# Attention and SwiGLU in one kernel: the first block takes its last pair late, and requests go ahead of staging copies

## The chip, the cores and the metric

The kernel runs on one core of a Trainium2 chip. The metric is device time in microseconds of the whole kernel. TensorE (PE) multiplies, VectorE (DVE) and ScalarE (ACT) work elementwise, GpSimd (POOL) copies within on-chip memory and asks for transfers, SyncE (SP) asks for other transfers, among them transposing ones. [...]

## The reference

Attention over 8 batches of 12 heads, 448 positions, 64 numbers per head; its output, heads side by side (3,584 rows of 768), goes through a gated feed-forward layer.

```python
scores = scale * np.matmul(q, k.transpose(0, 1, 3, 2))      # 8 x 12 x 448 x 448
attn = softmax(scores)
x = np.matmul(attn, v) -> (3584, 768)
g = x @ w_gate                                              # 768 x 1536
silu = g * (1.0 / (1.0 + np.exp(-g)))
out = (silu * (x @ w_val)) @ w_out                          # 1536 x 768
```

All inputs and the output are 32-bit floats; the kernel loads them as 16-bit floats (the conversion is done by the transfer).

## The kernel before

Heads are worked on in 48 pairs, six to a batch. A pair goes through these stages:

- **Loads.** `load_qk16` asks GpSimd's queue for queries and keys (L139), `load_v` for values (L156), `load_w` for parts of the three weights (L171). From pair 12 (`QUAD`) on, keys and values come in two requests each (`load_keys`, L127). The requests of one pair are called q14, k14, v12 and so on below; V3 stands for `load_v(9, 3)`, the values of pairs 9 to 11 in one request, and g, v, o are quarters of the gate and value weights and halves of the output weights.
- **Turning queries and keys.** Up to pair 10, TensorE transposes them (`turn`, L243). From pair 11 on, `prep` and `prep_quad` (L184, L199) let GpSimd copy keys and queries into a staging tile `qk16` (three buffers) and then ask SyncE's queue for transposing transfers into `qkT` (five buffers).
- **Scores.** `qk(pr, c)` multiplies (L293; L262 and L275 from pair 12 on) and ScalarE takes the exponential. Each pair has four chunks; from pair 12 on, two pairs have seven, the fourth (`RU`) holding the rest of both.
- **Values.** `copy_v` (L167) copies values on VectorE into a tile with a column of ones; `pv` multiplies (L319, L327; L356 from pair 12 on), and VectorE divides by the sum (L338, L340; L397, L398) into `xt`.
- **X.** `turn_x` transposes `xt` into the feed-forward input `X`: up to pair 11 on TensorE with a VectorE copy (L427, L434), later by a transposing transfer (L436).
- **Feed-forward.** Eight blocks of 384 or 512 rows. `ffn1_steps` (L460) has 12 steps, each with a gate group `gp` of 6 matmuls, a tanh on ScalarE (L480), a value group `vp` of 6 matmuls and two VectorE operations (L484, L487). `ffn2_steps` (L492) multiplies by the output weights in groups of 12 matmuls (L510).

PSUM holds three wide tiles (`ps_s`, two banks each) for scores and most gate groups, and two narrow ones (`ps_f`, one bank each) for everything else.

The order is written by hand. A first loop runs the 24 score chunks of pairs 0 to 5. The main loop then goes through `plan`, whose steps x hold two or three chunks and the pairs whose values are due. In the steps that matter here, the chunks are: x = 0 pair 6 (two chunks), x = 4 pair 8, x = 5 the last of pair 8 and two of pair 9, x = 6 pair 9 and the first of pair 10, x = 8 three of pair 11, x = 9 the last of pair 11 and two of pair 12, x = 10 two of pair 12 (one is the rest of 12 and 13) and one of pair 13, x = 11 two of pair 13 and one of pair 14.

When a step enters a pair `pr`, it prepares a later pair and asks for others: at pair 8 `prep(11)` and q14, k14; at pair 9 `prep(12)`, `prep(13)`, then q15, k15 and v12; at pair 10 `prep(14)`, then q16, k16 and v13; and so on. Other requests come from a table by pair, `wq` (L568). At x = 0 the last pieces of pairs up to 5 are finished (`piece`), `turn_x(5)` follows, and `add_block(0, end)` opens the first block, of 384 rows, all from batch 0. A gate group takes a narrow tile instead of a wide one when `gate_small` is set, which a step without values due (`bare`) does.

Of the kernel before, what the change touches and what calls it, by code (L numbers as in the profile page):

```python
# [10 lines left out]
FP32 = mybir.dt.float32  # L11
# [9 lines left out]
LA = 6  # L21
RB = 5
FIRST = 6
# [14 lines left out]
def kernel(  # L38
# [11 lines left out]
    B, H, S, D = q.shape  # L50
# [4 lines left out]
    NCB = DM // 128  # L55
    NFB = DF // 128
    NHP = H // 2
    NPAIR = B * NHP
# [29 lines left out]
    ps_f = ctx.enter_context(tc.tile_pool(name="ps_f", bufs=2, space=PSUM))  # L88
# [67 lines left out]
    def load_v(pr, n=1):  # L156
        b, h = divmod(2 * pr, H)
        if pr >= QUAD:
            vd = vraw[:, ds(pr % VS, n)].rearrange("p r h c d -> p (r h) (c d)")
            load_keys(nc.gpsimd, vd, v, 2 * pr, 2 * n)  # L160
            return
        nc.gpsimd.dma_start(
            vraw[0:P, ds(pr % VS, n)].rearrange("p r h c d -> p (r h) (c d)"),
            v[b, h : h + 2 * n].rearrange("h (p c) d -> p h (c d)", c=NC),
        )
# [291 lines left out]

    gate_small = [False]

    def ffn1_steps(kk, c0, n, hts):  # L460
        for fb in range(NFB):

            def group(kind, dst):
                for cb in range(NCB):
                    nc.tensor.matmul(  # L465
                        dst[:, 0:n],
                        lhsT=wslice(kind, fb, cb),
                        rhs=X[kk][:, cb, ds(c0, n)],
                        start=(cb == 0),
                        stop=(cb == NCB - 1),  # L470
                    )

            if gate_small[0]:
                gate_small[0] = False
                gp = ps_f.tile([128, 512], FP32, tag="f", name="gp")
            else:
                gp = ps_s.tile([128, 2, 512], FP32, tag="s", name="gp")[:, 0]
            group("g", gp)
            sg = fp.tile([128, 512], FP32, tag="sg")
            nc.scalar.activation(sg[:, 0:n], gp[:, 0:n], AF.Tanh, scale=0.5)  # L480
            vp = ps_f.tile([128, 512], FP32, tag="f", name="vp")
            group("v", vp)
            t1 = fp.tile([128, 512], FP32, tag="t1")
            nc.vector.scalar_tensor_tensor(  # L484
                t1[:, 0:n], sg[:, 0:n], 1.0, gp[:, 0:n], ALU.add, ALU.mult
            )
            nc.vector.scalar_tensor_tensor(  # L487
                hts[:, fb, 0:n], t1[:, 0:n], 0.5 * HS, vp[:, 0:n], ALU.mult, ALU.mult
            )
            yield  # L490

    def ffn2_steps(kk, c0, n, hts, first, last_block):  # L492
        chunks = range(n // 128)
        if first:
            steps = [(ch, oh) for oh in range(2) for ch in chunks]
        else:
            steps = [(ch, oh) for ch in chunks for oh in range(2)]
        osbs = {}
        for ch, oh in steps:
            last = last_block and ch == n // 128 - 1  # L500
            if last or oh == 0:
                osbs[ch] = fp.tile([128, DM], FP32, tag="osb", bufs=3, name="osb")
            osb = osbs[ch]
            parts = [(oh * OH, OH)]
            if last and oh:
                parts = [(OH, OH // 2), (OH + OH // 2, OH // 2)]
            for m0, w in parts:
                op = ps_f.tile([128, 512], FP32, tag="f")
                for fb in range(NFB):
                    nc.tensor.matmul(  # L510
                        op[:, 0:w],
                        lhsT=hts[:, fb, ts(ch, 128)],
                        rhs=wo[oh][:, fb, ds(m0 - oh * OH, w)],
                        start=(fb == 0),
                        stop=(fb == NFB - 1),
                    )
                nc.scalar.activation(osb[:, ds(m0, w)], op[:, 0:w], AF.Copy, scale=1.0 / HS)  # L517
                if not last:
                    m0, w = 0, DM
                    if oh == 0:  # L520
                        continue
                l0 = c0 + ch * 128
                l = l0
                while l < l0 + 128:
                    b, j = divmod(l, S)
                    turned = D if b + NB * kk < QUAD // NHP else 0
                    c, p0 = divmod((j + turned) % S, P)
                    m = min(P - p0, l0 + 128 - l, (MQ if turned and j < MQ else S) - j)
                    eng = nc.scalar if last and m < 64 else nc.sync
                    eng.dma_start(  # L530
                        out[ts(NB * kk + b, S), :].rearrange("(p c) m -> c p m", c=NC)[
                            c, p0 : p0 + m, ds(m0, w)
                        ],
                        osb[l - l0 : l - l0 + m, ds(m0, w)],
                    )
                    l += m
            yield NFB * OH / 2400.0

    def block(i):
        kk, odd = divmod(i, 2)  # L540
        c0, n = (384, 512) if odd else (0, 384)
        hts = hp_.tile([128, NFB, 512], FP16, tag="h")
        return ffn1_steps(kk, c0, n, hts), ffn2_steps(kk, c0, n, hts, i == 0, i == B - 1), n

    with tc.manual_schedule():
        load_qk32(0)
# [4 lines left out]
        for vo in Vts:  # L551
# [17 lines left out]
            0: [("qk", 6), ("g", 0), ("v", 0)],  # L569
            1: [("V", 2), ("qk", 8, 1), ("g", 1), ("v", 1)],  # L570
            3: [("qk", 9, 1), ("qk", 10), ("g", 2), ("v", 2)],
            4: [("g", 3), ("v", 3), ("qk", 12)],
            6: [("V", 3), ("o", 0)],
            7: [("o", 1)],
        }

# [75 lines left out]
        def piece():  # L652
            pv_chunk(*pieces.pop(0))

        for u in range(FIRST * NC):
            pr, c = divmod(u, NC)
# [33 lines left out]
        g = FIRST * NC  # L690
        last = len(units)
        while g < last or queue:
            n = 2 if g < WIDE * NC else 3
            todo = []
# [16 lines left out]
        for x, (chunks, todo) in enumerate(plan):  # L711
            quads = [u for u in chunks if u[0] >= QUAD and u[1] == RU]
            for pr, c in quads + [u for u in chunks if u not in quads]:
                qk(pr, c)
            for _, p0 in todo:
                if p0 >= QUAD:
                    pv_piece(p0, RU)
            end = min([y for y in adds if y > x] + [len(plan) + 1])
            if x == 0:
                turn_x(4)  # L720
                while pieces:
                    piece()
                turn_x(5)
                add_block(0, end)
            for p0 in vcopies.get(x, []):
                copy_v(p0)
            entered = [pr for pr, c in chunks if c == 0]
            for pr in entered:
                lead = [pr + 3] if pr + 3 < QUAD else [pr + 3, pr + 4] if pr + 3 == QUAD else [pr + 4]
                for p in lead:  # L730
                    if NPE <= p < NPAIR:
                        prep(p)
                if 14 <= pr + LA < NPAIR:
                    load_qk16(pr + LA, 1)
                if 12 <= pr + 3 < NPAIR:
                    load_v(pr + 3)
            for pr, c in chunks:
                if c == 2 and pr < NPE - 2:
                    prep(pr + 2)()
            if x in adds and x > 0:  # L740
                add_block(adds[x], end - x, x)
            for _, p0 in todo:
                pv(p0)
                if p0 < XPE:
                    turns.append(p0)
                else:
                    turn_x(p0)
            for pr in entered:
                for w in wq.pop(pr, []):
                    emit(w)  # L750
            bare = not todo and bool(chunks)
            if adds[max(y for y in adds if y <= x)] < 2:
                if bare and oq and not fvq:
                    carry -= run_o()
                elif bare:
                    gate_small[0] = True
                carry = run_budget(left() / (end - x) + carry)
            else:
                nf, no = steps.pop(0) if steps else (0, 0)
                if bare and no:  # L760
                    run_o()
                    no -= 1
                elif bare:
                    gate_small[0] = True
                for y in range(nf):
                    if fvq:
                        run_fv()
                for _ in range(no):
                    run_o()
            if x == 1:  # L770
                turn_rests(0)
            while turns:
                turn_x(turns.pop(0))
            if XPE - 1 in [p0 for _, p0 in todo]:
                turn_rests(1)
# [39 lines left out]
```

The softmax here doesn't subtract the row's maximum and nothing guards it: scores larger than these inputs give would overflow.

## Time and profile before

| | |
|---|---|
| time, median of 3 (lowest to highest) | 452.88 us (452.05 to 453.5) |
| span of the profiled run | 450.3 us, mean TensorE clock 0.999 |
| packets over the DMA queues | 108,494, 49.90 MB |
| GpSimd's queue (software) | 46,832 packets, 24.56 MB |
| SyncE's queue (hardware) | 61,520 packets, 24.66 MB |
| longest wait of GpSimd in sum | 96.5 us in 20 waits, staging copies at L188, for transposes into qkT |

The page of the profile gives the busy time of each engine as a share of the span, and a picture of 40 equal slices of about 11.3 us, one digit for each in tenths. The answers on waits name an instruction group, what released it, the total in us, the number of waits and the longest. In a timeline each line has a start and a length in us; in brackets stands the idle time of the engine before it and what seems to have ended it. For a wait on several semaphores the last one to come is named, which is not always the one that was missing.

### The profile page before, as it was taken

What the parts mean: (1) busy time and instruction counts of PE and PEld (TensorE: products, weight loads), DVE (VectorE), ACT (ScalarE), POOL (GpSimd) and SP (SyncE); (2) the same over time, 40 slices, a digit from 0 to 9 for tenths busy, and PEclk for the clock granted to TensorE, in tenths of its full rate; (3) what the DMA queues carried; (4) which work ended last, traced back from release to release, by engine and by line L of the source; (5) the groups of instructions that cost most, each with busy time, mean ns of one, the idle gap of its engine ahead of it and who ended that gap; (6) DMA issues with size and microseconds to landing.
All of it is one profiled execution on the core that took longest, in us unless ns stands there. A gap on an engine that the chain in (4) does not pass through costs nothing.

```text
span 450.3 us, 9959 instructions
## 1 busy us (share of the span) xinstructions
PE 438.5 (97%) x4024; PEld 247.0 (55%) x4024; DVE 199.9 (44%) x447; ACT 224.8 (50%) x332; POOL 180.4 (40%) x299
## 2 busy tenths in 40 slices
PE   8999999799999999999999999999999999999996
PEld 3655565444456566554556556554455656644464
DVE  4666562455564354344444434344544434045400
ACT  6965667545663654455536365454454651222222
POOL 8755715997786464336453366423000000000000
PEclk9999999999999999999999999999999999999999
DMA  9999999999998699975985797955141211200033
GB/s 137 182 199 201 199 177 144 138 160 217 135 148 104 110 144 124 125 115 69 120 109 105 111 140 96 151 84 94 32 79 47 52 41 22 80 27 1 0 107 105
DMA packets 108494, 49.90 MB, mean 111 GB/s; under 512 B 60832, under 2 KB 104992, under 8 KB 108448
## 3 DMA queue, kind: packets, MB, share of 16 engines
q0 software_dynamic: 46832, 24.56, 47.7%
q1 hardware_dynamic: 61520, 24.66, 29.0%
q8 instruction: 31, 0.51, 0.5%
q14 instruction: 15, 0.12, 0.1%
q10 hardware_dynamic: 96, 0.05, 0.0%
HBM read 49.55 MB, written 11.01 MB: 134 GB/s over the span
## 4 chain that ended last, share of the span: by engine, by line
PE 82%; DMA 9%; DVE 4%; ACT 2%; issue 1%; POOL 1%; SPq 0%; DVEq 0%; POOLq 0%
PE op L510 23%; PE gp L465 23%; PE vp L465 19%; PE acc L356 8%; DMA k<-in_k_dram 5%; PE s L262 4%; DMA q<-in_q_dram 2%; DVE t L484 2%; DVE hts L487 2%; PE s L293 1%; ACT sg L480 1%; PE acc L319 1%; DMA vraw<-in_v_dram 1%; PE s L275 1%; PE tp L252 1%
## 5 line engine op out<-in xcount | busy, mean ns | idle before, releaser
L465 PE MATMUL gp<-X,wg 128*128 128x384 f16 (+1 forms) x576 | 124.7, 353 | 0.0
L465 PE MATMUL vp<-X,wv 128*128 128x384 f16 (+1 forms) x576 | 124.6, 352 | 0.0
L510 PE MATMUL op<-wo,hts 128*128 128x384 f16 (+1 forms) x684 | 115.5, 323 | 1.4 <-DVE xt L398 1.4
L283 ACT ACTIVATE E<-s 128x896 f16<-128x896 f32 x126 | 106.5, 922 | 14.4 <-PE s L262 9.2
L484 DVE SCALAR_TENSOR_TENSOR t<-sg,gp 128x384 f32<-128x384 f32 (+1 forms) x96 | 59.6, 621 | 119.4 <-ACT sg L480 119.4
L480 ACT ACTIVATE sg<-gp 128x384 f32<-128x384 f32 (+1 forms) x96 | 52.6, 548 | 92.9 <-PE gp L465 91.4
L510 PEld LDWEIGHTS <-hts 128*128 128x128 f16 x684 | 65.9, 98 | 46.6 <-issue 2.2
L465 PEld LDWEIGHTS <-wv 128*128 128x128 f16 x576 | 56.3, 98 | 52.6
L517 ACT ACTIVATE osb<-op 128x384 f32<-128x384 f32 (+1 forms) x57 | 27.6, 484 | 103.5 <-PE op L510 99.7
L465 PEld LDWEIGHTS <-wg 128*128 128x128 f16 x576 | 53.4, 98 | 45.5 <-issue 0.7
L487 DVE SCALAR_TENSOR_TENSOR hts<-t,vp 128x384 f16<-128x384 f32 (+1 forms) x96 | 59.6, 621 | 10.8 <-PE rtp L449 0.5
L188 POOL COPY qk<-k 128x512 f16<-128x512 f16 x36 | 22.9, 637 | 98.6 <-DMA qkT<-qk 96.5
L132 POOL DMA_DIRECT2D vraw<-in_v_dram x72 | 44.1, 637 | 14.9 <-DMA k<-in_k_dram 6.9
L356 PE MATMUL acc<-vo,E 128*128 128x65 f16 (+1 forms) x1152 | 43.0, 193 | 1.7 <-DVE hts L487 1.4
L301 ACT ACTIVATE E<-s 112x896 f16<-112x896 f32 x48 | 40.7, 917 | 7.8 <-PE s L293 7.5
L356 PEld LDWEIGHTS <-E 128*128 128x128 f16 (+1 forms) x1152 | 37.2, 96 | 12.8 <-issue 7.1
L132 POOL DMA_DIRECT2D k<-in_k_dram x70 | 42.5, 623 | 2.1 <-DMA wv<-in_moe_w_val_dram 0.7
L397 DVE RECIPROCAL R<-acc 128x4 f32<-128x4 f32 x68 | 12.1, 177 | 61.3 <-PE acc L356 61.2
L151 POOL DMA_DIRECT2D q<-in_q_dram x44 | 29.9, 678 | 5.0 <-PE s L293 1.6
L398 DVE TENSOR_TENSOR xt<-acc,R 128x256 f16<-128x256 f32 x68 | 28.9, 425 | 2.3
L262 PE MATMUL s<-qkT 64*128 64x448 f16 x216 | 28.1, 353 | 0.5 <-DMA qkT<-qk 0.5
L188 POOL COPY qk<-q 112x512 f16<-112x512 f16 x36 | 23.4, 651 | 0.0
(56 smaller groups left out, 185.4 us busy)
## 6 DMA issues: line engine op xcount, KB each, us to landing
vraw<-in_v_dram POOLq DMA_DIRECT2D x72, 64.0 KB, 4.8
q<-in_q_dram POOLq DMA_DIRECT2D x41, 112.0 KB, 3.7
k<-in_k_dram POOLq DMA_DIRECT2D x68, 64.0 KB, 4.5
wg<-in_moe_w_gate_dram POOLq DMA_DIRECT2D x8, 288.0 KB, 10.0
wv<-in_moe_w_val_dram POOLq DMA_DIRECT2D x8, 288.0 KB, 10.1
wo<-in_moe_w_out_dram POOLq DMA_DIRECT2D x2, 1152.0 KB, 20.1
out_dram<-osb SPq DMA_DIRECT2D x8, 288.0 KB, 3.7
out_dram<-osb SPq DMA_DIRECT2D x6, 336.0 KB, 2.9
```

Source lines behind the costliest of these rows:

```text
L132: eng.dma_start(dst[ts(s, 64)], rows)
L151: nc.gpsimd.dma_start(dst[0:P, ds(h0, 2 * n)], flat.rearrange("h (p c) d -> p h (c d)", c=NC))
L188: nc.gpsimd.tensor_copy(dst.rearrange("p c h d -> p h c d"), src)
L262: nc.tensor.matmul(s[:, hx, 0:S], lhsT=t[ts(hx, 64), ts(c + low(pr, hx), 128)], rhs=t[ts(hx, 64), ds(NC * 128, S)], start=True, stop=True,)
L283: nc.scalar.activation(e[:, 0 : 2 * S].rearrange("p (h q) -> p h q", h=2), s[:, :, 0:S], AF.Exp, scale=sm_scale)
L301: nc.scalar.activation(e[:, :, 0:S], s[0:P, :, 0:S], AF.Exp, scale=sm_scale)
L356: nc.tensor.matmul(accs[pr][0][hx][:, ts(j, D + 1)], lhsT=e[rows, ds(hx * S + j * 128, 128)], rhs=Vts[pr % NV][rows, hx, col, 0 : D + 1], ...
L465: nc.tensor.matmul(dst[:, 0:n], lhsT=wslice(kind, fb, cb), rhs=X[kk][:, cb, ds(c0, n)], start=(cb == 0), stop=(cb == NCB - 1),)
L480: nc.scalar.activation(sg[:, 0:n], gp[:, 0:n], AF.Tanh, scale=0.5)
L484: nc.vector.scalar_tensor_tensor(t1[:, 0:n], sg[:, 0:n], 1.0, gp[:, 0:n], ALU.add, ALU.mult)
L487: nc.vector.scalar_tensor_tensor(hts[:, fb, 0:n], t1[:, 0:n], 0.5 * HS, vp[:, 0:n], ALU.mult, ALU.mult)
L510: nc.tensor.matmul(op[:, 0:w], lhsT=hts[:, fb, ts(ch, 128)], rhs=wo[oh][:, fb, ds(m0 - oh * OH, w)], start=(fb == 0), stop=(fb == NFB - 1),)
```

## The change

It has three parts.

1. At x = 0, `turn_x(5)` is no longer ahead of the first block. The first step of `ffn1_steps` takes it in between: five of six gate matmuls (those that need pairs 0 to 4), `turn_x(5)`, five of six value matmuls, then the sixth of each. The first gate group takes a wide tile, since x = 0 no longer counts as bare. It is for the wait of TensorE for pair 5's division.
2. V3 is asked for at pair 4, ahead of q12 and k12, instead of at pair 6.
3. When a pair is entered, the requests for later queries, keys and values are written ahead of the staging copies of `prep`, so that the requests go out earlier.

```diff
-    def ffn1_steps(kk, c0, n, hts):
+    def ffn1_steps(kk, c0, n, hts, late=None):
...
-            def group(kind, dst):
-                for cb in range(NCB):
+            def group(kind, dst, cbs=range(NCB)):
+                for cb in cbs:
...
-            group("g", gp)
+            split = late and fb == 0
+            if split:
+                vp = ps_f.tile([128, 512], FP32, tag="f", name="vp")
+                group("g", gp, range(NCB - 1))
+                late()
+                group("v", vp, range(NCB - 1))
+                group("g", gp, [NCB - 1])
+            else:
+                group("g", gp)
             sg = fp.tile([128, 512], FP32, tag="sg")
             nc.scalar.activation(sg[:, 0:n], gp[:, 0:n], AF.Tanh, scale=0.5)
-            vp = ps_f.tile([128, 512], FP32, tag="f", name="vp")
-            group("v", vp)
+            if split:
+                group("v", vp, [NCB - 1])
+            else:
+                vp = ps_f.tile([128, 512], FP32, tag="f", name="vp")
+                group("v", vp)
...
+        late = (lambda: turn_x(FIRST - 1)) if i == 0 else None
...
-            4: [("g", 3), ("v", 3), ("qk", 12)],
-            6: [("V", 3), ("o", 0)],
+            4: [("g", 3), ("v", 3), ("V", 3), ("qk", 12)],
+            6: [("o", 0)],
...
-                turn_x(5)
                 add_block(0, end)
...
             for pr in entered:
+                if 14 <= pr + LA < NPAIR:
+                    load_qk16(pr + LA, 1)
+                if 12 <= pr + 3 < NPAIR:
+                    load_v(pr + 3)
                 lead = [pr + 3] if pr + 3 < QUAD else [pr + 3, pr + 4] if pr + 3 == QUAD else [pr + 4]
                 for p in lead:
                     if NPE <= p < NPAIR:
                         prep(p)
-                if 14 <= pr + LA < NPAIR:
-                    load_qk16(pr + LA, 1)
-                if 12 <= pr + 3 < NPAIR:
-                    load_v(pr + 3)
...
-            bare = not todo and bool(chunks)
+            bare = not todo and bool(chunks) and x > 0
```

More of the change, by code (lines that the diff above doesn't have):

```diff
@@ L542, in block @@
         hts = hp_.tile([128, NFB, 512], FP16, tag="h")
-        return ffn1_steps(kk, c0, n, hts), ffn2_steps(kk, c0, n, hts, i == 0, i == B - 1), n
+        late = (lambda: turn_x(FIRST - 1)) if i == 0 else None
+        return ffn1_steps(kk, c0, n, hts, late), ffn2_steps(kk, c0, n, hts, i == 0, i == B - 1), n
     with tc.manual_schedule():
```

## The prediction

> **What bounds the kernel now.** I read the shares of busy time first, then the slices, then TensorE's waits, and last the timelines of GpSimd and TensorE around the few places where TensorE stands still.
>
> ```profile
> PE 438.5 (97%) x4024; PEld 247.0 (55%) x4024; DVE 199.9 (44%) x447; ACT 224.8 (50%) x332; POOL 180.4 (40%) x299
> ...
> DMA  9999999999998699975985797955141211200033
> ```
>
> TensorE is busy for 97% of the 450.3 us span, so the whole idle time that a change can win is 11.8 us. The DMA row says where trouble can come from: the 16 DMA engines are full in the first 13 slices (up to about 70 us) and not after slice 21. The table by stretch confirms it: from 84 to 450 us TensorE is idle for 4.9 us in 366, from 72 to 84 us for 2.3 us in 12.
>
> ```profile
> PE op L510 <- DVE xt L398: 1.4, 1, 1.4
> PE acc L356 <- DVE hts L487: 1.4, 7, 0.2
> PE wp L116 <- DVE warm L547: 1.2, 1, 1.2
> PE acc L427 <- DVE xt L340: 1.0, 1, 1.0
> ...
> PE s L262 <- DMA qkT<-qk: 0.5, 1, 0.5
> ```
>
> Three of these waits matter here. The 1.0 us at L427 is `turn_x(5)` of step x = 0 waiting for the division of pair 5 (TensorE idle 28.7 to 29.66). The 0.5 us at L262 is the first score chunk of pair 14, waiting for a transpose at 80.58. The 1.4 us at L510 ends at 83.33: the output group needs the accumulator of pair 12, whose division sits on VectorE behind `copy_v(13)`, which waited for values until 81.81.
>
> GpSimd's timeline shows why those values are late (columns: start, length, engine, line, operation, idle before it and what ended it):
>
> ```profile
> 47.14 2.04 POOL L182 DMA_DIRECT2D wo<-in_moe_w_out_dram x2 [1.33 <-issue]
> 49.17 0.63 POOL L211 COPY qk<-q 112x512 f16<-112x512 f16 x1
> ...
> 53.41 0.61 POOL L188 COPY qk<-k 128x512 f16<-128x512 f16 x1 [0.77 <-DMA k<-in_k_dram]
> ...
> 56.36 1.20 POOL L132 DMA_DIRECT2D k<-in_k_dram x2
> 64.39 0.59 POOL L132 DMA_DIRECT2D vraw<-in_v_dram x1 [6.84 <-DVE R L338]
> 71.93 0.59 POOL L132 DMA_DIRECT2D vraw<-in_v_dram x1 [6.94 <-DMA k<-in_k_dram]
> 73.14 0.61 POOL L188 COPY qk<-k 128x512 f16<-128x512 f16 x1 [0.62 <-DMA k<-in_k_dram]
> ```
>
> The requests at 64.39 and 71.93 are the two halves of `load_v(12)`. The releasers named are not the cause. The two `wo` requests landed as follows (asked for at 47.14 and 48.17):
>
> ```profile
> wo<-in_moe_w_out_dram POOLq DMA_DIRECT2D x1, 1152.0 KB, 16.7
> wo<-in_moe_w_out_dram POOLq DMA_DIRECT2D x1, 1152.0 KB, 23.5
> ```
>
> That is 63.84 and 71.67: each half of v12 went out 0.3 to 0.5 us after one of them. Counting GpSimd's requests in order, `wo` 0 and 1 are numbers 44 and 45, v12's halves 52 and 53; the records name eight completion semaphores in turn, and earlier pairs fit (request 24 at 20.47 follows the landing of 16 at 20.2; 39 at 38.81 that of 31 at 38.5). So a request waits until the one eight before it has landed, and GpSimd, being in order, holds everything behind it. In the kernel before, only the copies of pair 14 were behind v12.
>
> [...] while transposes ran (54 to 62 us) the software queue moved about 0.145 MB/us, without them 0.197. [...] Here only the start shows the slow state (7 warm-up matmuls of 512 columns in 3.17 us, against 1.46 us for 6 later).
>
> **The change, part by part.**
>
> Part 1, the first gate group. Before: pieces end at 28.70, wait to 29.66, three transposes 0.18, then 24 matmuls in two pairs of groups. After: five gate matmuls (a group of six takes 0.97, so 5 x 0.162 = 0.81 us) fill 28.71 to 29.52; the transposes still wait for the division (29.61), so 0.14 us of the wait stays; five value matmuls cover 29.84 to 30.65, just over the copy of X (30.04 to 30.60); the last two end at 30.98. Before, that was 31.79: 0.8 us won. The tanh still starts at 31.0. Moving this `gp` to the wide score buffers costs nothing: the score three tiles earlier has left its buffer before 28.7, and the freed small bank lets `vp` start.
>
> Part 2, values of 9 to 11 before the query and keys of 12. The 336 KB go ahead of 480 KB; nothing waits for these values (they landed at 54.7, first copied at 57.6), so it wins nothing. But V3 becomes request 40, and request 48 (second half of k14, now ahead of `prep(11)`) waits for it. V3 lands near 50.3 + 0.34 MB / 0.2 = 52.1, so pair 11's copies move from 49.17 to about 53.0; its transposes, asked for at 54.1 and 56.1 with the 9.7 us that they took before, land at 63.8 to 65. TensorE wants them at 65.3. Cost 0 to 1 us, and what it costs is covered by the next part.
>
> Part 3, requests ahead of copies. At pair 9 the order becomes q15, k15, v12, then the copies of 12 and 13. v12 is still request 52 and 53, so it still waits for both `wo`. The copies that ran from 53.41 to 55.7 now come after the landing of `wo` 1. Behind them stand four transposes on the sync queue, and TensorE, in order, wants pair 12 at 72.2 and pair 13 at 74.75.
> - When does `wo` 1 land? 2.36 MB from 54.1 us. With nothing beside it: 66.6. As before, with six transposes: 71.67. Now only pair 11's 0.245 MB run beside it: 3.5 us at 0.197 (0.69 MB), 5.2 us at 0.145 (0.75), the last 0.92 to 1.02 MB at 0.197 (5.0): 68.0, and I allow 0.4 for the dip seen at 62 to 64 us. I take 68.4.
> - v12's second half at 68.65, first copy at 69.25 (0.6 per request). First copy done 69.85; transposes leave the sync queue each 1.25 us (they took 1.2 each, a little apart): 69.9, 71.15, 72.4, 73.7.
> - Landing: those of pairs 14 to 16 took 4.0 to 6.2 us with loads beside them. With 5.5 and 5.8: q12 at 76.65, q13 at 79.5.
> - TensorE: pair 12's first chunk at 76.65 instead of 72.2; with two chunks (0.55) and an output group (2.05) it reaches 79.2 and waits for q13: chunk (12, rest) at 79.5 instead of 74.75. That is 4.75 us late, and the 0.8 us of part 1 is swallowed, since an absolute time sets it.
> - Given back: q16, k16, v13 are asked for at 71.4 to 74.4, pair 14's copies follow at 74.4, its transposes land near 82, and TensorE comes there at 84: the 0.5 us wait goes. v13 lands near 79, so the 1.43 us shrinks to the 0.2 that the division itself needs: together 1.7 us.
>
> Sum: 4.75 - 0.49 - 1.23 = +3.0 us. After 84 us GpSimd's copies wait for qkT buffers (96.5 us over 20 times) and the DMA engines have room, so later requests a copy earlier are hidden, and TensorE passes the 3 us on to the end. 452.88 + 3.1 = 456.0 us (the tenth for part 2).
>
> **The rivals.**
> - Even: `wo` 1 lands at its floor, 66.6, and transposes take 4 to 4.5 us; q13 then lands at 71.9 + 4.5 = 76.4, 1.7 us late, which the 1.7 us given back cancel: 452.9. For it: transposes at 73.78 took 4.0. Against: pair 11's transposes must still run beside `wo`.
> - Faster: the requests do not hold the copies, or the copies' delay stays inside the slack. Then 0.8 + 1.7 = 2.5 us are won: 450.4. For it: the three waits are real. Against: it needs q13 before about 74.7 and q12 before 72, under even the floor, or another order of semaphores than the one that fits every earlier request.
> - Later: `wo` 1 lands at 71.67 as before: everything 3.3 us later, 459.3[...]
>
> **How the numbers follow.** Main 0.58, later 0.22, even 0.12, faster 0.08. The range takes the main case, the edge of the even one and most of the later one: 452.6 to 460.0. Slower by over 0.3% (above 454.2): main, later and a little of the even case, 0.82; within 0.3%: 0.11; faster: 0.07.
>
> **What would show it.** Right: v12's halves leave 0.3 us after the `wo` landings, the four copies of 12 and 13 at about 69 instead of 53 to 55, TensorE waiting at L262 for qkT by 4 us or more near 72 us and again near 79, no 1.4 us wait at L510, the wait at L427 down to 0.1 to 0.2. Wrong: copies of pair 12 before 60 us, or no wait at L262 over 1 us. If the copies are late but the total is even, it is the landing times that I have wrong; if the clock record shows half speed after 72 us, the later case.

## The result and the profile after

| | before | after |
|---|---|---|
| median (lowest to highest), 6 runs each | 452.47 us (450.69 to 454.14) | 456.69 us (455.5 to 457.48) |
| ratio, 95% interval | | 1.0091 (1.0062 to 1.012) |
| span of the profiled run, mean TensorE clock | 450.3 us, 0.999 | 454.5 us, 0.991 |

The changed kernel is slower by 0.9%, about 4.1 us. The forecast was 456.0 us.

The first lines are those of the page of the kernel after: busy time by engine, and the granted TensorE clock in 40 slices.

```profile
PE 441.1 (97%) x4024; PEld 247.4 (54%) x4024; DVE 198.3 (44%) x447; ACT 225.2 (50%) x332; POOL 180.4 (40%) x299
...
PEclk9999997999999999999999999999999999999999
```

The same 4,024 matmuls were busy for 2.6 us longer, and one slice (68 to 80 us) has a granted clock of 0.7. Next, the waits of TensorE in the kernel after (total us, times, longest):

```profile
PE s L262 <- DMA qkT<-qk: 3.7, 1, 3.7
PE acc L356 <- DVE hts L498: 1.5, 8, 0.2
PE wp L116 <- DVE warm L559: 1.2, 1, 1.2
...
PE s L293 <- DMA qkT<-qk: 0.5, 1, 0.5
...
PE op L521 <- DVE xt L398: 0.4, 1, 0.4
```

The 1.0 us at L427 has gone, the 1.4 us at the output group is down to 0.4, and a wait of 3.7 us for transposes has come. GpSimd's timeline in the kernel after:

```profile
46.87 2.05 POOL L182 DMA_DIRECT2D wo<-in_moe_w_out_dram x2 [1.78 <-issue]
...
53.41 0.70 POOL L211 COPY qk<-q 112x512 f16<-112x512 f16 x1
...
61.45 0.59 POOL L132 DMA_DIRECT2D vraw<-in_v_dram  x1 [4.99 <-DVE t L495]
68.83 0.59 POOL L132 DMA_DIRECT2D vraw<-in_v_dram  x1 [6.78 <-DMA wo<-in_moe_w_out_dram]
69.41 0.62 POOL L188 COPY qk<-k 128x512 f16<-128x512 f16 x1
```

The two requests for v12 still leave after the landings of the two weight halves, now at about 61 and 68.5, and the copies of pairs 12 and 13, which ran from 53.41 before, begin at 69.41. GpSimd started nothing in the 4.99 and 6.78 us ahead of the two requests, though the queries and keys for those copies had landed by 54.7. Last, the chain that ended last, in order of time (start, length, what):

```profile
47.90 20.65 DMA wo<-in_moe_w_out_dram
...
68.83 0.41 POOL vraw L132
...
69.41 1.21 POOL qk L188 x3
...
71.33 4.17 DMA qkT<-qk
...
75.53 0.93 PE s L262 x4
76.46 3.95 PE op L521 x12
80.42 0.52 PE s L275 x4
```

It names every link that the forecast put together: second weight half, second half of v12, copies, transposes, pair 12's scores. One link is longer than forecast: the output group at 76.46 takes 3.95 us, where 12 such matmuls take 2.1.

### The profile page after: what moved, and what is told of

The parts are those of the page before. It is cut to its first block, busy times and chain, and to the rows that moved or that the text cites. A ratio compares the mean times of both kernels' runs of the same rounds, so it can differ in the third digit from the quotient of the medians.

```text
span 454.5 us, 9930 instructions
## 1 busy us (share of the span) xinstructions
PE 441.1 (97%) x4024; PEld 247.4 (54%) x4024; DVE 198.3 (44%) x447; ACT 225.2 (50%) x332; POOL 180.4 (40%) x299
## 4 chain that ended last, share of the span: by engine, by line
PE 78%; DMA 13%; DVE 3%; POOL 2%; ACT 1%; issue 1%; DVEq 0%; POOLq 0%
PE op L521 24%; PE gp L465 21%; PE vp L465 19%; PE acc L356 8%; DMA wo<-in_moe_w_out_dram 5%; DMA wv<-in_moe_w_val_dram 4%; PE s L262 4%; DMA wg<-in_moe_w_gate_dram 2%; DVE hts L498 1%; DVE t L495 1%; ACT sg L488 1%; PE s L275 1%; DMA vraw<-in_v_dram 1%; DMA qkT<-qk 1%; POOL k L151 1%
## 5 line engine op out<-in xcount | busy, mean ns | idle before, releaser
L521 PE MATMUL op<-wo,hts 128*128 128x384 f16 (+1 forms) x684 | 117.4, 327 | 0.4 <-DVE xt L398 0.4
L262 PE MATMUL s<-qkT 64*128 64x448 f16 x216 | 28.3, 357 | 3.7 <-DMA qkT<-qk 3.7
```

Source lines behind the costliest of these rows:

```text
L262: nc.tensor.matmul(s[:, hx, 0:S], lhsT=t[ts(hx, 64), ts(c + low(pr, hx), 128)], rhs=t[ts(hx, 64), ds(NC * 128, S)], start=True, stop=True,)
L521: nc.tensor.matmul(op[:, 0:w], lhsT=hts[:, fb, ts(ch, 128)], rhs=wo[oh][:, fb, ds(m0 - oh * OH, w)], start=(fb == 0), stop=(fb == NFB - 1),)
```

## The experiments

Each version was timed beside the kernel before on the same chip. The chip differs between groups of versions, so versions are best compared by their ratios. Output-weight halves are called o0 and o1.

**Part 1 alone** (the split group; order and table as before).

> Part 1 alone (the split first group; order of requests and table as before). My theory: the wait at L427 falls from 1.0 to 0.1 us, but TensorE at 79 to 83 us waits for things that land at absolute times (a transpose of pair 14 at 80.6, values of pair 13 at 81.7), so the waits there grow by what was won: total within 0.3% of before, gain 0 to 0.3 us, and the wait at the output group after L398 grows from 1.4 to about 2.2 us. Rival (the won 0.8 us reaches the end): about 451.7, waits at 79 to 83 us as before.

Measured: 452.21 us, ratio 1.0001 (0.9976 to 1.0026). The gain did not reach the end, as expected, but the sign given for it did not come: in this profile the wait at the output group is 1.3 us, not 2.2. The timelines tell why. First the kernel before, then part 1 alone (start, length; the scores of steps 0 and 1, and the output group at the end of the stretch):

```profile
27.03 0.55 PE L293 MATMUL s<-qkT 64*128 64x448 f16 x4
...
33.83 0.55 PE L293 MATMUL s<-qkT 64*128 64x448 f16 x4
...
83.33 4.08 PE L510 MATMUL op<-wo,hts 128*128 128x384 f16 x24 [1.43 <-DVE xt L398]
```

```profile
28.66 0.55 PE L293 MATMUL s<-qkT 64*128 64x448 f16 x4
...
34.65 0.55 PE L293 MATMUL s<-qkT 64*128 64x448 f16 x4
...
83.52 2.77 PE L521 MATMUL op<-wo,hts 128*128 128x384 f16 x16 [1.33 <-DVE xt L398]
```

From step 0 to step 1 part 1 needs 5.99 us instead of 6.80: the 0.8 us are real. But this run began the stage 1.63 us later, was still 0.82 us behind at step 1, and at the output group is only 0.19 us behind. The request for v12's second half leaves at 72.00 us here and at 71.93 before, whatever TensorE has done. That fits waits that end with landings and not with how early TensorE comes; the runs below that move o1 test it.

**Part 2 alone** (V3 ahead of q12 and k12).

> Part 2 alone (V3 ahead of q12 and k12). My theory: nothing waits for V3, so no change, 452.5 within 0.5 us; copies of pairs 12 and 13 begin about 1.4 us later than 53.4 because k12 lands later. Rival (the slower time of the changed kernel comes from q12 and k12 being pushed back): 1 us or more slower.

Measured: 452.53 us, ratio 0.9995 (0.9976 to 1.0014). Copies of pairs 12 and 13 began at 55.47 instead of 53.41, 2.1 us later. The weights were asked for 0.73 us later in this run (47.87 instead of 47.14), so about 1.3 us are the change's, near the 1.4 expected. Nothing came of it.

**Part 3 alone** (requests ahead of copies, at every pair).

> Part 3 alone (requests ahead of copies at every pair). My theory: it holds the whole loss, since the landing of the second output-weight half sets an absolute time: 456 to 457.5 us, copies of pairs 12 and 13 at about 69, a wait at L262 of about 3 to 4 us near 72, TensorE at half clock behind it. Rival (the loss needs V3's move as well, or part 1): under 454.

Measured: 456.87 us, ratio 1.009 (1.0057 to 1.0123): the whole loss. In its profile, of the slowest of six runs, the copies begin at 70.16, and the wait is in two pieces, 2.2 us at L262 and 2.4 us at L275. The granted clock is 1.00 from 72 to 82 us and 0.79 on average from 82 to 90: half speed shows only after the second wait, so the clock is not what starts the loss.

**One pair's order alone**: the kernel before with pair 9's requests first.

```diff
+                if pr == 9:
+                    requests()
                 lead = ...
                 for p in lead:
                     if NPE <= p < NPAIR:
                         prep(p)
+                if not (pr == 9):
+                    requests()
```

> The kernel before with one edit: at pair 9 alone, q15, k15 and v12 ahead of the copies of pairs 12 and 13. My theory: this one change of order is enough for the whole loss: copies of 12 and 13 at about 69 to 70, a wait of 2 to 4 us at L262 near 72, 456 to 457.5 us, ratio near 1.009. Rival (the order at the other pairs, 8 and 10 above all, carries part of it): 453.5 to 455.

Measured: 455.79 us, ratio 1.0078 (1.0052 to 1.0104). Waits of TensorE and GpSimd's timeline in this run:

```profile
PE s L262 <- DMA qkT<-qk: 4.9, 1, 4.9
```

```profile
67.82 0.59 POOL L132 DMA_DIRECT2D vraw<-in_v_dram  x1 [5.30 <-DMA wo<-in_moe_w_out_dram]
68.41 0.62 POOL L188 COPY qk<-k 128x512 f16<-128x512 f16 x1
```

Four copies moved behind five requests at one place make up 3.5 of the 4.1 us; the intervals of this run and of the full change overlap. The time is just under the 456 to 457.5 expected and above the rival's 455. The wait of 4.9 us is longer than the 2 to 4 expected, but this is the profile of the second slowest of ten runs.

**The changed kernel with the old order at pair 9 alone** (`pr != 9` in the edit above).

> The changed kernel with the old order at pair 9 alone (copies of 12 and 13 ahead of q15, k15, v12). My theory: copies of 12 and 13 at about 55, no wait over 1 us near 72, no half clock. The copies of pair 14 now stand behind v13's requests, which follow v12's second half at about 72, so they start at 75.5 instead of 73.1 and pair 14 lands at about 82.9: a wait of 2 to 3.5 us at L262 near 79 takes the place of the waits at 79 to 83. Total 452.5 to 454. Rival (pair 9 is the whole difference and the rest of the change brings its 2.5 us): 450.

Measured: 453.63 us, ratio 1.0019 (1.0001 to 1.0036). The loss goes nearly to nothing, and no gain comes back, as expected. The reason was half missed. In the profile the wait that took the place is 1.2 us at L275 for pair 13, and pair 14 cost only 0.5 us; pair 11's copies started at 52.64 there instead of 49.17, ahead of those of 12 and 13, which probably pushed their transposes back. "No half clock" was missed too. The profile is of the fastest of 22 runs, one of five at a mean clock of 0.999 or more (median 452.5 us); the other 17 have a mean clock of 0.992 to 0.996 and a median of 454.0, and no trace shows their waits.

**Requests first everywhere, but v12 asked for ahead of o0 and o1.**

```diff
-            6: [("o", 0)],
+            6: [("V12", 12), ("o", 0)],
...
-                if 12 <= pr + 3 < NPAIR:
+                if 13 <= pr + 3 < NPAIR:
```

> The changed kernel (requests ahead of copies everywhere) with v12 asked for at pair 6, ahead of the output weights, so that the requests at pair 9 no longer wait for them. My theory: copies of 12 and 13 at about 57 to 60 although requests still go first, no wait over 1.5 us near 72, no half clock; q16 and k16 of pair 10 now stand eight behind the weight halves, so pair 14's copies start at about 75 and a wait of 1 to 3 us stays near 80: 452.5 to 454.5 us. Rival (requests ahead of copies cost as such, whatever they wait for): 456 or more.

Measured: 452.38 us, ratio 0.9999 (0.9979 to 1.0019). Requests still go first, the copies of 12 and 13 begin at 58.45, and the loss is gone. So it is not the order as such that costs, but what the requests ahead of the copies wait for. The remaining wait came at another place than expected: 2.5 us at L293 for pair 11, whose copies started at 55.52. Half clock, which was not expected, follows it from about 69.2 to 72.6 us (mean granted clock 0.92 from 54 to 72 us, 0.98 from 72 to 90).

**The clock.** Sixteen matmuls on a zero tile ahead of pair 12's first chunk in the changed kernel.

```diff
+                if (pr, c) == (QUAD, 0):
+                    dummy(16)
                 qk(pr, c)
```

> The changed kernel with 16 warm-up matmuls of 512 columns ahead of pair 12's first score chunk, to keep TensorE at full clock over the wait. My theory: the output group after the wait takes 2.1 us instead of 4.0, but TensorE then waits for pair 13's transposes, which land at 79.8, so only 0.5 to 0.8 us come back: about 456.0 us, clock 0.999, a wait of about 1 us at L275. Rival (the half clock is paid in full): 1.9 us or more come back, under 455.

Measured: 455.16 us, ratio 1.0055 (1.0034 to 1.0077). It was run again beside the changed kernel:

> The changed kernel again, beside the next one on one chip: 456 to 457.5 us, mean clock 0.991 to 0.996.

> The changed kernel with the 16 warm-up matmuls, beside the run of the changed kernel alone: the difference is what the half clock costs. My theory: 0.5 to 1.0 us less. Rival (paid in full, 1.9 us for the output group and more for the score chunks): 2 us less.

Measured: changed kernel 456.47 us, ratio 1.0097 (1.0077 to 1.0117); with the extra matmuls 455.5 us, ratio 1.0082 (1.0055 to 1.0109). Busy time, granted clock (the third number from the end), DMA share and GB/s by stretch, first in the profile of the kernel after, then with the extra matmuls (second timing):

```profile
76.00:78.00 2.00, 2.00 (x10) 0.77 (x7) 0.00 (x0) 1.73 (x2) 2.00 (x4) 0.50 1.69 149
78.00:80.00 2.00, 2.00 (x8) 0.88 (x6) 0.00 (x0) 0.00 (x0) 2.00 (x5) 0.50 1.82 127
```

```profile
76.00:78.00 2.00, 1.78 (x12) 0.71 (x10) 0.00 (x0) 0.73 (x1) 2.00 (x4) 1.00 1.40 134
78.00:80.00 2.00, 1.78 (x11) 0.84 (x9) 0.00 (x0) 1.48 (x3) 2.00 (x5) 1.00 1.42 174
```

The half clock is gone in this stretch, and the medians fall by 1.0 us side by side (456.47 to 455.5), and by 1.5 us from the result's 456.69 to 455.16. The first is at the upper end of what was expected, the second above it. The intervals of the ratios overlap, so the size is not settled; neither pair of medians reaches the 1.9 us of the rival. The profiles fit that: at full clock TensorE waits again for pair 13 (1.1 us at L275 in the first of these runs, 0.5 in the second).

The medians of the kernel before are themselves a mixture. Over its 130 runs in these groups, 91 have a mean clock of 0.998 or more and a median of 452.0 us, 39 one of 0.996 or less and a median of 453.9. All 12 runs of the changed kernel lie at 0.996 or less. Those 1.9 us are no price of the clock, because a longer wait can both cost time and be followed by a lower clock, as the 3.7 us in the profile after were; they show that even small differences of medians depend on how many runs lost it.

**What sets 79 to 83 us: moving o1.** Part 1, old order, and o1 asked for later. First at pair 9:

```diff
-            7: [("o", 1)],
+            9: [("o", 1)],
```

> Part 1 with the table and the order as before, but the second output-weight half is asked for at pair 9, behind v12, instead of at pair 7. My theory: v12 and the requests behind it no longer have a weight half eight requests ahead of them that lands at 72; v12's second half waits for the first weight half only (about 62 to 64 us), copies of pair 14 start at about 65 to 66, v13 is asked for by 68. All three waits at 79 to 83 us shrink (L398 from 1.4 to 0.4, L262 gone), and part 1's 0.8 us reaches the end: 449.7 to 450.7 us, ratio 0.994 to 0.996. The second half must land before about 75.5 us, when TensorE first wants it. Rival (DMA bandwidth, not the order, sets 79 to 83 us): within 0.3% of before, with a wait for wo near 76.

Measured: 453.02 us, ratio 1.0002 (0.9987 to 1.0017). The rival was right on the time. The waits of TensorE in the profiled run:

```profile
PE op L521 <- DMA wo<-in_moe_w_out_dram: 2.4, 1, 2.4
PE acc L356 <- DVE hts L498: 1.5, 8, 0.2
```

The old waits shrank as expected, but o1, asked for at 66.05, took 11.9 us and landed at 77.95; TensorE had come for it at 75.6. I had allowed it to 75.5. Ten of the 22 runs, the profiled one among them, kept a mean clock of 0.998 or more and have a median of 451.6 us; the other twelve, at 0.995 or 0.996, have 453.3. Next at pair 8 (`8: [("o", 1)]`):

> Part 1 with the order as before and the second output-weight half asked for at pair 8, behind q14 and k14 (one pair later than before, one earlier than in the run with it at pair 9). My theory: k14 lands at about 64 instead of 73, so copies of pair 14 start at about 65; v12's second half waits for q14 (about 64) and not for the weight half; v13 is held only by the weight half at about 72 and goes out at 73 instead of 76; the half itself lands by about 73, ahead of TensorE. Waits at 79 to 83 us down to 0.4 us each, part 1's 0.8 us reaches the end: 449.7 to 450.8 us, ratio 0.994 to 0.997. Rival (bytes alone set 79 to 83 us, whatever the order): within 0.3% of before, with a wait for wo or for values that takes the place.

Measured: 450.48 us, ratio 0.9968 (0.9952 to 0.9985). This is within the range expected, 0.3% faster than the kernel before (the interval leaves out 1) and faster than the changed kernel. How much of it is part 1's was not run apart. A new wait of 1.6 us remained, for pair 11's division: it stands on VectorE behind `copy_v(12)`, and v12, queued behind o1, landed at 77.3 to 77.7. The last version asks for v12 ahead of o1 at pair 8 and no longer at pair 9:

> The run before (part 1, second output-weight half at pair 8) with v12 asked for ahead of that half. There v12 landed at 77.4 behind the half, and the division of pair 11, standing behind copy_v(12) on VectorE, held TensorE for 1.6 us. My theory: v12 now lands by about 67, the 1.6 us fall to under 0.5 us, the half lands 0.7 us later at about 75.3, just as TensorE comes for it (wait 0 to 0.5 us): 449.0 to 450.2 us, ratio 0.993 to 0.996. Rival (the bytes decide, so a wait for the half takes the place): ratio as in that run, 0.997, with a wait for wo of 1 to 2 us.

Measured: 450.65 us, ratio 0.9963 (0.9944 to 0.9983), within the interval of the run before it. That is the rival's time, above the 449.0 to 450.2 us expected, yet without the wait for o1 that the rival named. The 1.6 us are gone from the profile:

```profile
78.88 0.38 PE L449 MATMUL rtp<-ident,xt 128*64 128x64 f16 x12 [0.41 <-ACT osb L528]
81.39 4.07 PE L521 MATMUL op<-wo,hts 128*128 128x384 f16 x24 [0.37 <-DVE xt L398]
85.40 0.88 PE L275 MATMUL s<-qkT 64*64 64x448 f16 x4
```

These are the only waits left from 70 to 85 us, and the output group comes at 81.39 instead of 83.33. But the next score chunk (85.40), the rest of pairs 14 and 15, takes 0.88 us where it took 0.38 before: half a microsecond is lost within it. The wait view doesn't name the cause; the chain that ended last (window 74 to 90 us) does:

```profile
65.54 11.47 DMA k<-in_k_dram
...
79.75 6.11 DMA qkT<-qk
...
85.90 0.38 PE s L275 x3
```

It is pair 15's transpose, landed at 85.86. The keys of pair 15, asked for behind o1, took 11.5 us, so their copies began only at 77.83. That the bytes of o1 ahead of them are the reason is my estimate; no run shows it.

## Why the prediction was right, step by step

- **Requests wait for the landing eight before.** Right. In the traces before and after, GpSimd's 219 requests name eight semaphores in strict turn. None leaves before the one eight ahead has landed (0.28 us behind it at the least); 33 requests before and 40 after leave within 0.7 us of it. Not tested by changing the number of semaphores; what the runs add is that v12's halves follow o0 and o1 in the changed kernel, and that moving v12 ahead of them frees the copies.
- **The landing of o1.** I took 68.4 us; it was 47.9 + 20.65 = 68.5. My sum was a little off: its own parts give 54.1 + 3.5 + 5.2 + 5.0 = 67.8, not 68.0, and 2.36 MB at 0.197 end at 66.1, not 66.6. The 0.4 us allowed on top brought it near.
- **Copies and transposes.** First copy forecast 69.25, measured 69.41. q12 forecast at 76.65, measured 71.33 + 4.17 = 75.5: its transpose took 4.2 us, not 5.5. q13 forecast at 79.5, measured 73.94 + 5.9 = 79.8. The 4.0 to 6.2 us that I read before were medians of one or two transposes; single ones took 4.0 to 7.0.
- **TensorE at the chunk with pair 13.** Forecast 79.5, measured 80.35: 5.6 us late instead of 4.75. Here the sum was too small. Of the 0.85 us, 0.34 are q13's landing (79.84). The other 0.51 are the half clock: the output group took 4.0 us instead of 2.1 and so outlasted that landing. I had half speed only as a sign of the rival "later" (0.22), and that it could come there was not shown: in the trace before, the slow matmuls that I named stand at the start. It belongs in the main case.
- **Given back at 79 to 83.** Forecast 1.7 us, measured 5.60 - 4.22 = 1.4: the two waits shrank by 0.5 and 1.06 us, and 0.2 us went to score chunks still at half clock. From 83 us on TensorE passes 4.22 us on to the end: 446.51 to 450.73 for its last matmul.
- **Part 1.** 0.8 us won where it is made (6.80 to 5.99) and nothing at the end, with the change and alone. The forecast said the first; the second follows from its own reading of the waits at 79 to 83 us as landings.
- **Part 2.** No effect alone. Together with part 3 it delays pair 11's copies to 53.41 (forecast 53.0), but most of that is part 3's: alone it had them at 53.08, in a run 0.75 us later at the weights; the wait of 0.5 us at L293 is inside the 0 to 1 us forecast.
- **The rivals.** "Faster" fell with the first timing. "Even" fell because o1 landed at 68.5 and not at 66.6, and q13's transpose took 5.9 us and not 4 to 4.5. Of "later", the landing at 71.67 did not come (68.5), but half clock did, and taking it away won 1.0 us in the medians side by side.
- **The signs.** Of those listed for "right", the wait at L262 was 3.7 us instead of 4 or more, and none came near 79 us, because the slow output group filled that stretch. The sign listed for "later", half speed after 72 us, did come, at 74.12 us, without the later landing; 456.7 us is nearer to my main case (456.0) than to that rival (459.3).
- **The room on the DMA engines.** I read the first 13 slices as 70 us; at 11.3 us each they end at 146, so that row doesn't show the engines free from 70 us on. The table by stretch serves better: the DMA share that it gives is 1.34 from 40 to 72 us, 1.23 to 84, and 0.66 after.

The size is then 4.1 to 4.2 us instead of the 3.1 us forecast. The missing term is mainly the clock: 0.5 us ahead of pair 13 and 0.2 after it in the profile, 1.0 to 1.5 us in the medians; q13's landing adds 0.3. That the forecast of 456.0 comes within 0.7 us of 456.69 owes 0.4 us to luck, since I built it on 452.88 and the six runs before have 452.47.

## What to carry to other kernels

On an engine that both copies and asks for transfers, look in the trace for requests that wait: here they held GpSimd for 5.0 and 6.8 us, and the copies behind them moved from 53.41 to 69.41. Before moving a request ahead of work that is ready, look up which earlier request carries the same semaphore (here always the one eight before) and when that one lands. A wait removed from the busiest engine pays only if the next thing it meets is its own work: part 1 alone stayed at 452.21 us. Where the next waits end on landings, move the transfers first (450.48 us with o1 at pair 8 as well), and look at what each moved transfer pushes back. Waits of 2.4 to 4.9 us on TensorE were followed by half clock in four profiles here, and one of 2.4 us was not, so price the clock with the wait and look at the clock of every run, not of the profiled one alone.

## What was not expected of the hardware

The clock fell sooner than I expected. In the changed kernel the record of the granted clock drops to half at 74.12 us, 2.3 us after the last matmul ended at 71.86 and before the next began at 75.53. It stays there for 6.83 us, through more than five microseconds in which TensorE was busy without a break. By stretch in the kernel after (stretch, length, TensorE's busy time; the clock is the third number from the end):

```profile
72.00:74.00 2.00, 0.00 (x0) 0.09 (x1) 0.58 (x3) 0.82 (x1) 2.00 (x4) 1.00 0.57 82
74.00:76.00 2.00, 0.47 (x4) 0.13 (x3) 0.00 (x0) 0.00 (x0) 2.00 (x5) 0.53 1.56 159
...
80.00:82.00 2.00, 2.00 (x31) 0.89 (x30) 0.00 (x0) 1.50 (x3) 2.00 (x4) 0.76 1.51 192
82.00:84.00 2.00, 2.00 (x28) 1.35 (x25) 0.83 (x2) 1.52 (x2) 2.00 (x5) 1.00 1.43 205
```

The length of a wait did not tell by itself whether the clock would fall. Waits of TensorE over 2 us in five profiled runs, and the mean granted clock around them:

| run | wait, and when it ended | granted clock |
|---|---|---|
| kernel after | 3.67 us, 75.53 | 0.53 from 74 to 76 us, 0.50 to 80, 0.76 to 82 |
| pair 9's order alone | 4.90 us, 77.53 | 0.993 over the run; 12 output matmuls behind the wait took 3.98 us instead of 2.1 |
| part 3 alone | 2.15 us, 75.97; 2.42 us, 81.31 | 1.00 from 72 to 82 us, 0.79 to 90 |
| v12 ahead of o0 and o1 | 2.50 us, 67.58 | 0.92 from 54 to 72 us, 0.98 to 90 |
| o1 at pair 9 | 2.37 us, 77.97 | 1.00 from 54 to 84 us |

Of these waits the one for o1 at pair 9 and the first of part 3 alone were not followed by a lower clock in the stretches shown. Twelve other runs of the version with o1 at pair 9 had a mean clock of 0.995 or 0.996, and left no trace. What makes the difference was not shown: no run moved a wait in time on purpose.

Transposes took longer while the software queue moved more. Those asked for between 50 and 60 us in the kernel before took 8 to 13 us to land, with 1.67 MB moved by that queue in those 10 us; those between 71 and 80 us took 4 to 7 us, with 0.81 MB in those 9. The queue need not be the whole reason. The first six followed each other closely, and four in a row in the changed kernel, from 70 us on, took 2.4, 4.2, 5.2 and 5.9 us, each longer than the one ahead of it. No run parts the two.
